# Loading the first feed-forward weights as eight loads of unequal row counts in place of four whole ones, in a one-core decode block

## The chip, the cores and the metric

The kernel runs on one core of one Trainium2 chip. The metric is the device time of one execution, in microseconds (us). The kernel before took 1313.02 us as the median of three runs (1312.45 to 1314.26). All tensors are float32.

## The reference, cut to what matters

One decode step of a transformer block, for two sequences (B = 2) and one new token each. The widths are D = 512, 32 heads of 128, a key and value cache of 8192 positions, and a feed-forward width of F = 1792.

```python
def _A_ref(x, k_cache, v_cache, wq, wo):          # x is layernorm(input)
    q = (x @ wq).reshape(B, 1, 32, 128).transpose(0, 2, 1, 3)
    scores = einsum("bhqd,bhkd->bhqk", q, k_cache) * 128 ** -0.5
    o = einsum("bhqk,bhkd->bhqd", softmax(scores), v_cache)
    return o.transpose(0, 2, 1, 3).reshape(B, 1, 4096) @ wo

def _B_ref(x, w1, b1, w2, b2):                    # x is layernorm(h)
    h = relu(x @ w1 + b1) ** 2
    return h @ w2 + b2

h  = x + _A_ref(layernorm(x), k_cache, v_cache, wq, wo)
h2 = h + _B_ref(layernorm(h), w1, b1, w2, b2)
```

The weights `wq` and `wo` have 8 MB each, `w1` and `w2` 3.67 MB each, and the two caches together 537 MB: 64 pairs of a head and a sequence with 4 MB of keys and 4 MB of values each.

## The kernel before, in words

SBUF holds a ring of three slots, each 128 partitions by 16384 floats (8 MB). One slot takes the keys and the values of one pair, or `wq`, or `wo`. The 64 pairs are worked one after the other by a loop over `i`. `front(i)` makes the scores of pair `i` with 32 matmuls (line 156), takes their maximum on VectorE (line 158) and their exponential on ScalarE (line 159). `back(i)` multiplies the values with them in four passes on VectorE of 2048 columns each, whose sums are the pair's unnormalised output (`weighted`, line 165). Every load is issued by the SyncE queue (SP), in the order of the program.

The end of the program differs from the loop. Slot 0 takes `wo`, in two halves (line 61). Pair 62, the last but one, goes to slot 1. The last pair, 63, goes to slot 2: its keys as one load (line 227), then its values as five (line 234, the fourth quarter in two parts). After the scores of pair 63 and the last pass over the values of pair 62 the program issues the feed-forward weights into slot 1. `W1`, a view of 4 blocks of 1792 columns, takes the place of the keys of pair 62: one load of 128 rows for each block (line 251), where a row is 1792 contiguous floats, 7168 bytes. `W2` is 14 blocks of 512 columns and takes the next columns of the slot, in five loads of 4, 4, 3, 2 and 1 blocks (line 254).

A load into a place must wait until the instructions that read what was there are done. Besides, the framework gives the loads eight completion semaphores in turn: load number n of the program uses semaphore n mod 8, and it is not issued before load n - 8 has landed. SP waits for this ahead of the issue, and whatever stands behind it on SP waits too. Counted in the program, the four loads of `W1` are numbers 73 to 76 and wait for pair 62 (65), the keys of pair 63 (66), the second half of `wo` (67) and the first quarter of the values of pair 63 (68). The five of `W2` are numbers 77 to 81 and wait for the second and third quarters, the two parts of the fourth, and the first load of `W1`. The store of the result is number 82 and waits for the second load of `W1`.

When the last pair is done, the tail runs: its part of the output (lines 195 and 196), the projection with `wo` (lines 203, 212 and 274), the second layernorm (lines 102 to 114), the first feed-forward matmuls, 32 records in 4 blocks of `W1` (line 281), the transposition and squared relu on VectorE (lines 287 to 292), the second feed-forward matmuls, 112 records in 14 blocks of `W2` (line 295), and the store (line 299). The first matmul of a block waits for that block's load.

Of the kernel before, what the change touches and what calls it, by code (L numbers as in the profile page):

```python
# [25 lines left out]
BLK = 512  # L26
GROUPS = [(0, 16), (16, 31), (31, 32)]
W2_PIECES = [4, 4, 3, 2, 1]
EPS = 1e-5
SCALE = DH ** -0.5  # L30

# [2 lines left out]
def attention_block_kernel(ctx: ExitStack, tc: tile.TileContext, small, kvd, wqd, wod, w1d, w2d, out):  # L34
    nc = tc.nc
# [18 lines left out]
    W1 = ring[:, 1, : DB * F].rearrange("p (d c) -> p d c", d=DB)  # L54
# [21 lines left out]
    eps_t = consts.tile([P, 1], F32, name="eps_t")  # L76
    nc.vector.memset(eps_t, EPS)
    zero = consts.tile([P, 1], F32, name="zero")
# [169 lines left out]
    sl = front(last)  # L248
    weighted(last - 1, s, NH - 1, 0, CS, AC[:, last - 1, NH - 1 : NH])
    for d in range(DB):  # L250
        nc.sync.dma_start(W1[:, d], w1d[:, d])
    at = 0
    for n in W2_PIECES:
        nc.sync.dma_start(W2[:, at : at + n], w2d[:, at : at + n])
# [75 lines left out]
```

## Time and profile before

| What | us |
|---|---|
| median of the three runs | 1313.02 |
| the profiled execution | 1314.19 |
| its span in the profile | 1312.4 |
| the DMA engines' busy share over the span | 99.0% |
| VectorE busy | 729.7 (56%) |
| TensorE busy | 415.3 (32%) |
| ScalarE busy | 143.8 (11%) |
| moved by DMA | 561 MB at 428 GB/s |

The profiled execution stands 1.8 us above its span, which is the time around the span that the profile doesn't show, and 1.17 us above the median. The chain in the profile is the chain of work that ended last, followed back from the end; where it names a DMA, the instruction behind it had waited for that load to land. A line with SPq is SP's queue, issuing or waiting. PEclk is the clock that TensorE was granted, as a share of full speed.

### The profile page before, as it was taken

What the parts mean: (1) busy time and instruction counts of PE and PEld (TensorE: products, weight loads), DVE (VectorE), ACT (ScalarE), POOL (GpSimd) and SP (SyncE); (2) the same over time, 40 slices, a digit from 0 to 9 for tenths busy, and PEclk for the clock granted to TensorE, in tenths of its full rate; (3) what the DMA queues carried; (4) which work ended last, traced back from release to release, by engine and by line L of the source; (5) the groups of instructions that cost most, each with busy time, mean ns of one, the idle gap of its engine ahead of it and who ended that gap; (6) DMA issues with size and microseconds to landing.
All of it is one profiled execution on the core that took longest, in us unless ns stands there. A gap on an engine that the chain in (4) does not pass through costs nothing.

```text
span 1312.4 us, 6090 instructions
## 1 busy us (share of the span) xinstructions
PE 415.3 (32%) x2476; PEld 121.8 (9%) x2476; DVE 729.7 (56%) x633; ACT 143.8 (11%) x149; POOL 0.7 (0%) x6
## 2 busy tenths in 40 slices
PE   3523323313322322322332332332332232233355
PEld 0300000000000000000000000000000000001113
DVE  1455665564565566466556556556556655655743
ACT  1111011011011101101101101101110110110111
POOL 0000000000000000000000000000000000000000
PEclk9666566666667666666666656656665666675766
DMA  9999999999999999999999999999999999999996
GB/s 416 416 445 428 433 445 420 441 424 439 430 430 442 425 441 430 431 434 428 436 427 441 432 433 430 437 428 433 435 432 431 434 439 422 443 429 434 428 417 265
DMA packets 11979, 561.45 MB, mean 428 GB/s; under 512 B 1456, under 2 KB 1584, under 8 KB 2736
## 3 DMA queue, kind: packets, MB, share of 16 engines
q1 hardware_dynamic: 11952, 561.07, 99.0%
q8 instruction: 19, 0.31, 0.1%
q14 instruction: 8, 0.07, 0.0%
HBM read 561.00 MB, written 0.07 MB: 428 GB/s over the span
## 4 chain that ended last, share of the span: by engine, by line
DMA 63%; DVE 20%; PE 12%; ACT 4%; issue 1%; SPq 0%; DVEq 0%; ACTq 0%
DMA ring<-in_kvd 62%; DVE ring L165 15%; PE s L156 9%; DVE NM L158 4%; ACT s L159 3%; DMA ring<-in_wqd 2%; PE s L139 1%; PE s L133 1%; PE s L203 0%; PE s L281 0%; PE s L295 0%; DVE QR L142 0%; PE s L274 0%; PE s L212 0%; ACT big L135 0%
## 5 line engine op out<-in xcount | busy, mean ns | idle before, releaser
L165 DVE SCALAR_TENSOR_TENSOR ring<-ring,s 128x2048 f32<-128x2048 f32 (+1 forms) x257 | 570.5, 2276 | 135.7 <-ACT s L159 135.7
L156 PE MATMUL s<-ring,QR 128*32 128x512 f32 x2048 | 361.8, 871 | 832.2 <-DMA ring<-in_kvd 789.5
L158 DVE TENSOR_REDUCE NM<-s 128x1 f32<-128x2048 f32 x64 | 146.7, 2292 | 382.6 <-PE s L156 382.6
L159 ACT ACTIVATE s<-s,NM 128x2048 f32<-128x2048 f32 x64 | 124.3, 1942 | 1081.5 <-DVE NM L158 1081.5
L156 PEld LDWEIGHTS s<-ring,QR 128*32 128x32 f32 x2048 | 91.1, 153 | 1100.4 <-issue 1093.5
L142 DVE TENSOR_SCALAR QR<-s 128x2048 f32<-128x2048 f32 x1 | 2.3, 2291 | 38.5 <-PE s L139 38.5
L165 DVE DVE_READ_ACCUMULATOR ring<-ring,s 128x1 f32 x257 | 21.4, 83 | 0.0
L133 PE MATMUL s<-ring,xn 128*2 128x512 f32 x64 | 8.9, 703 | 18.8 <-DMA ring<-in_wqd 18.0
L203 PE MATMUL s<-ring,OT 128*2 128x512 f32 x62 | 11.6, 900 | 9.8 <-ACT s L97 5.9
L159 ACT ACTIVATION_READ_ACCUMULATOR s<-s,NM 128x1 f32 x64 | 12.3, 193 | 0.0
L139 PE MATMUL s<-ident,big 128*128 128x2 f32 x64 | 10.9, 307 | 0.8 <-ACT big L135 0.8
L139 PEld LDWEIGHTS s<-ident,big 128*128 128x128 f32 x64 | 10.8, 270 | 1.7 <-issue 1.7
L184 PE MATMUL s<-lw,pick_all 128*128 128x32 f32 (+2 forms) x6 | 1.9, 394 | 14.6 <-DVE lw L183 14.6
L97 ACT ACTIVATE s<-zero 128x512 f32<-128x512 f32 (+2 forms) x6 | 3.2, 532 | 19.8 <-DVE OT L196 10.7
L281 PE MATMUL s<-ring,xc 128*2 128x448 f32 x32 | 5.0, 794 | 0.4 <-ACT rstd L113 0.4
L176 PE MATMUL s<-NM,pick 128*128 128x32 f32 (+2 forms) x24 | 4.0, 310 | 3.3 <-DVE hT L213 2.6
L176 PEld LDWEIGHTS s<-NM,pick 128*128 128x128 f32 x24 | 3.7, 236 | 5.3 <-issue 3.5
L135 ACT ACTIVATE big<-s 128x512 f32<-128x512 f32 x2 | 1.2, 598 | 26.8 <-PE s L133 26.8
L103 PE MATMUL s<-part,ones_d 128*128 128x2 f32 x8 | 2.3, 363 | 5.2 <-ACT s L97 3.4
L133 PEld LDWEIGHTS s<-ring,xn 128*2 128x2 f32 x64 | 1.6, 92 | 25.2 <-issue 23.5
L203 PEld LDWEIGHTS s<-ring,OT 128*2 128x2 f32 x62 | 2.0, 110 | 18.9 <-issue 12.1
L295 PE MATMUL s<-ring,a 128*2 128x128 f32 x112 | 3.2, 273 | 1.4 <-DVE a L292 1.4
(59 smaller groups left out, 38.4 us busy)
## 6 DMA issues: line engine op xcount, KB each, us to landing
ring<-in_wod SPq DMA_DIRECT2D x2, 4096.0 KB, 42.1
ring<-in_kvd SPq DMA_DIRECT2D x1, 4096.0 KB, 32.7
ring<-in_w1d SPq DMA_DIRECT2D x4, 896.0 KB, 20.3
ring<-in_kvd SPq DMA_DIRECT2D x3, 1024.0 KB, 38.5
ring<-in_w2d SPq DMA_DIRECT2D x2, 1024.0 KB, 16.6
ring<-in_kvd SPq DMA_DIRECT2D x2, 512.0 KB, 38.3
ring<-in_kvd SPq DMA_DIRECT2D x63, 38.9
ring<-in_w2d SPq DMA_DIRECT2D x1, 768.0 KB, 17.6
```

What stands on the lines that cost most here:

```text
L97: nc.scalar.activation(ap, zero.to_broadcast([P, n]), AF.Copy)
L103: nc.tensor.matmul(pm, ones_d, part, start=True, stop=True)
L133: nc.tensor.matmul(bk[k][32 * j : 32 * j + B, :], xn[:, d, :], WQ[:, d, n * BLK : (n + 1) * BLK], start=(d == 0), stop=(d == DB - 1))
L139: nc.tensor.matmul(bk[2][:, h * B : (h + 1) * B], big[:, at : at + DH], ident[:, 32 * j : 32 * j + B], start=True, stop=True)
L156: nc.tensor.matmul(bk[n][32 * j : 32 * j + 32, :], QR[:, i, :], keys(i)[:, j, n * BLK : (n + 1) * BLK], start=True, stop=True)
L158: nc.vector.tensor_reduce(NM[:, i : i + 1], s, axis=AX.X, op=ALU.max, negate=True)
L159: nc.scalar.activation(s, s, AF.Exp, bias=NM[:, i : i + 1], scale=1.0, accum_out=LS[:, i : i + 1])
L165: nc.vector.scalar_tensor_tensor(v, v, 1.0, s[:, lo:hi], op0=ALU.mult, op1=ALU.mult, accum_out=acc)
L176: nc.tensor.matmul(pn[:, j], pick[:, j, :], NM[:, a:b], start=True, stop=True)
L203: nc.tensor.matmul(hp[32 * j : 32 * j + B, :], OT[:, h * B : (h + 1) * B], WO[:, h, :], start=(h - h0 < NQ), stop=(h1 - h <= NQ))
L281: nc.tensor.matmul(y[32 * j : 32 * j + B, :], xc[:, d, :], W1[:, d, j * FQ : (j + 1) * FQ], start=(d == 0), stop=(d == DB - 1))
L295: nc.tensor.matmul(o[32 * j : 32 * j + B, :], a2[:, m, :], W2[:, m, j * P : (j + 1) * P], start=False, stop=(m == FB - 1))
```

## The change

Each of the four loads of `W1` is issued as two, cut by rows (partitions): rows 0 to 119 and 120 to 127 of the first block, 104 and 24 rows of the second, 88 and 40 of the third, 72 and 56 of the fourth. The bytes, their places and the order of the blocks stay. No compute instruction is added or removed.

```diff
 W2_PIECES = [4, 4, 3, 2, 1]
+W1_CUTS = [120, 104, 88, 72]
...
     for d in range(DB):
-        nc.sync.dma_start(W1[:, d], w1d[:, d])
+        cut = W1_CUTS[d]
+        nc.sync.dma_start(W1[:cut, d], w1d[:cut, d])
+        nc.sync.dma_start(W1[cut:, d], w1d[cut:, d])
     at = 0
     for n in W2_PIECES:
         nc.sync.dma_start(W2[:, at : at + n], w2d[:, at : at + n])
```

With four loads more, the numbers behind the first of them move, and with them the semaphores. In the program after, `W1` is loads 73 to 80, which wait for loads 65 to 72: pair 62, the keys of pair 63, the second half of `wo`, and the five loads of the values of pair 63. `W2` is loads 81 to 85, which wait for the first five loads of `W1` (120, 8, 104, 24 and 88 rows), and the store waits for the sixth (40 rows). On TensorE the first matmul of each block of line 281 waits for two loads in place of one. The order of the instructions on each engine is otherwise the same.

## The prediction

> **What bounds the kernel now.** I read the page first: the span, the DMA row of the slices and the shares of the chain.
>
> ```profile
> span 1312.4 us, 6090 instructions
> DMA  9999999999999999999999999999999999999996
> DMA 63%; DVE 20%; PE 12%; ACT 4%; issue 1%; SPq 0%; DVEq 0%; ACTq 0%
> ```
>
> The DMA engines are full until the last fortieth, so the loop is bound by the caches' 537 MB. The change touches nothing issued before load 73, so only the end counts. There the chain in order of time shows which wait ends last:
>
> ```profile
> 1226.67 29.79 DMA ring<-in_kvd
> 1256.46 0.14 issue
> 1256.59 6.54 PE s L156 x32
> ...
> 1287.14 4.49 DVE ring L165 x6
> ...
> 1299.46 5.03 PE s L281 x32
> 1304.49 0.27 PE s L285 x8
> ...
> 1305.91 0.20 DVE a L292
> 1306.11 0.04 issue
> 1306.15 3.28 PE s L295 x112
> ```
>
> The last DMA on the chain is pair 62, landing at 1256.46. From there to the end it is 53 us of compute: neither line 281 (`W1`) nor line 295 (`W2`) follows a DMA. Third, the queue: SP's timeline, then its own waits from 1250 us on.
>
> ```profile
> 1263.03 15.77 SPq L251 DMA_DIRECT2D ring<-in_w1d  x4
> 1280.96 7.48 SPq L254 DMA_DIRECT2D ring<-in_w2d  x5
> ```
>
> ```profile
> SPq L251 <- DMA ring<-in_kvd: 13.8, 3, 8.9
> SPq L254 <- DMA ring<-in_kvd: 6.0, 4, 2.1
> SPq L299 <- DMA ring<-in_w1d: 1.8, 1, 1.8
> SPq L254 <- DMA ring<-in_w1d: 1.8, 1, 1.8
> ```
>
> SP issues each load late, when the load eight before it lands. Last, the stretches of the tail (columns: busy time of PE, PEld, DVE, ACT, POOL, then granted clock, DMA share, GB/s):
>
> ```profile
> 1292.00:1296.00 4.00, 3.24 (x22) 3.10 (x22) 0.34 (x3) 0.00 (x0) 0.00 (x0) 0.50 1.00 416
> 1296.00:1300.00 4.00, 2.49 (x12) 1.80 (x16) 1.01 (x7) 0.26 (x1) 0.00 (x0) 0.50 0.81 328
> 1300.00:1302.00 2.00, 2.00 (x16) 0.44 (x12) 0.00 (x0) 0.00 (x0) 0.00 (x0) 0.50 0.45 174
> 1302.00:1304.00 2.00, 2.00 (x20) 0.43 (x16) 0.00 (x0) 0.00 (x0) 0.00 (x0) 0.70 0.10 41
> 1304.00:1306.00 2.00, 0.71 (x16) 0.13 (x8) 1.11 (x4) 0.00 (x0) 0.00 (x0) 1.00 0.00 0
> ```
>
> The transfers don't stop together: the share falls from 1.00 to 0.81, 0.45 and 0.10, so some DMA engines are done about 5 us before the others, and all are idle by 1304.3, ahead of line 295.
>
> **Cover of each load.** Asked load by load, the four issues of line 251 start at 1263.0, 1266.2, 1276.0 and 1278.5 and land 25.1, 24.1, 16.5 and 16.2 us later: 1288.1, 1290.3, 1292.5, 1294.7. Line 281 takes a block of `W1` every 5.03/4 = 1.26 us from 1299.46, the fourth at 1303.2, so the covers are 11.4, 10.4, 9.5 and 8.5 us. The five issues of line 254 land at 1297.1, 1300.5, 1302.3, 1303.6 and 1304.2 (the last 1288.1 + 16.1). Line 295 takes 3.28 us for 14 blocks and reaches the pieces (after 0, 4, 8, 11, 13 blocks) at 1306.15, 1307.1, 1308.0, 1308.7, 1309.2. Covers: 9.0, 6.6, 5.7, 5.1 and 5.0 us. The smallest, 5.0 us of the last piece, is what the change may use up for nothing.
>
> **The change part by part.**
>
> *Four more issues on SP*, 0.33 us each by line 251's records: 1.3 us. Behind them on SP stand only `W2` and the store, and SP spends these stretches waiting. Nothing.
>
> *The issues of `W2` come later.* The first piece now waits for the 120-row load instead of the second value quarter: about 1288.1 instead of 1281.0, if the 120 rows land when the first block did. The fifth waits for the 88-row load, at about the third block's landing, 1292.5, plus what the loads ahead gained; before it was 1288.1. A queue that runs dry costs time. At 1288.1 the engines that are behind still have three blocks queued: 2.75 MB at 428 GB/s is 6.4 us, and an issue to an idle queue lands after 1.5 us (the store's row). At the fifth issue they still have a third of a block and the fourth, about 2.8 us. So the engines that finish last never run dry; one with few rows of `W1` may, but from 1289.6 it needs only 3.67 MB at 428 GB/s, 8.6 us, for all of `W2`, and is done by 1299 or so. Nothing.
>
> *The store* waits for the sixth load of `W1`, before 1300 in every case below but the dear one, against 1309.8. Nothing.
>
> *Four more waits on TensorE*, ahead of line 281's blocks, for loads long landed. Low end nothing, since the waits can run ahead of the pipelined matmuls; high end the 0.14 us "issue" behind a DMA wait at line 156, 0.6 us together. I take 0.1: the other "issue" rows are 0.02 to 0.04.
>
> *The rows on the DMA engines.* Bytes are the same, but a load that isn't 128 rows need not fill sixteen engines evenly. The trace of before has no such load, so I bound it. At 428/16 = 26.75 GB/s per engine a 7168-byte row takes 0.268 us; a block is 8 rows per engine, all of `W1` 32. Low end: still 32, nothing (an engine that is late may even get fewer, but an earlier landing is worth nothing under cover). High end: the larger load keeps 8 rows on an engine and the smaller one puts another 8 on that same engine, four times: 64 rows, 32 x 0.268 = 8.6 us more. I take the smaller loads spread as the 128-row ones are: 1 + 2 + 3 + 4 rows on the busiest engine, 42 in all, 10 x 0.268 = 2.7 us, because every load that the trace shows completes in sixteen parts. Then the last `W1` lands at 1297.4 (needed 1303.2) and the last of `W2` at 1306.9 (needed 1309.2): 2.3 us of cover are left, and the end doesn't move. At the high end the last piece lands at 1312.8 and the end moves 3.6 us.
>
> [...]
>
> **Sum.** 0.1 us, from the waits on TensorE. The profiled execution would go from 1314.19 to 1314.3; the median of the runs lies 1.17 us below it: 1313.1, which I round up to 1313.2.
>
> **The rivals.**
>
> *Slower: the cut loads move more slowly, and the last piece of `W2` comes too late.* [...] For it: at 1.00 DMA share and 26.75 GB/s per engine nothing is to spare, and no row shows an unevenly shared load. Against it: the five value loads and `W2` pieces of four sizes all keep that rate. If each row took twice as long, 42 rows would be 22.5 us in place of 8.6: 13.9 more, less 5.0 of cover, 8.9 us, 1322. Between no slowing and that, the high end of the row count alone gives 3.6 us, 1316.7. It decides from 5.0 us of extra work on the engine that ends last, and passes 0.2% (2.6 us) from 7.6: `W1` taking 16.2 us there in place of 8.6. Chance 0.26, around 1317.
>
> [...]
>
> *Faster: TensorE gets its clock earlier in the tail.* In the stretches above it is granted 0.50 until 1302, and 1.00 only from 1304. Line 281's 5.03 us at nearly half clock could become 2.5, and lines 212 and 274 (1.88 each) half: 4.4 us at most, 1308.8. Against it: the change gives the clock no cause, and the spread of the three runs, 1.8 us, contains such luck already. With 2.6 us needed, chance 0.1. The same luck the other way (line 295 at half clock, 3.3 us, 1316.4) has 0.04.
>
> *The cut changes nothing in the engines' shares*: the forecast again, 1313.0, and inside it.
>
> **How the numbers follow.** A difference below 0.2%, 2.6 us, is about what a measurement of this kernel can't tell from none. Forecast and the do-nothing case, 0.60: 1313.2, within 1311.5 and 1315. Slower rival 0.26 and late clock 0.04 give slower 0.30; faster 0.10. The range goes up to 1318.0, over the high end of the rows (1316.7) and part of the slowing, leaving out 0.1, and down to 1310.8, leaving out 0.07.
>
> **What would show it.** Right: SP's timeline has eight issues at line 251/254 of the new kernel from 1263 on; the first `W2` issue moves to about 1288; the DMA share decays longer, with 1304 to 1307 not at zero; TensorE's `W2` matmuls still follow VectorE on the chain, 53 us after pair 62's landing. Wrong: the chain shows a DMA ahead of `W1`'s or `W2`'s matmuls; `W1` rows that take much more than 0.27 us; or a chain that differs before 1263, which I hold untouched.

## The result, and the profile after

The changed kernel takes 1326.84 us (median of four runs, 1325.96 to 1327.29) against 1313.36 us for the kernel before (median of the three runs of the table and one more): 1.010 times as long, 95% interval 1.0088 to 1.0112, or 13.5 us more. The forecast was 1313.2 in a range of 1310.8 to 1318.0. The profiled execution took 1326.43 us at a span of 1324.7, 12.3 more than the span before.

The page of the kernel after: the span, the slices, and the chain by line.

```profile
span 1324.7 us, 6097 instructions
DMA  9999999999999999999999999999999999999996
GB/s 412 434 422 440 439 420 438 441 420 437 438 432 430 435 438 429 429 438 432 428 437 430 432 441 428 439 428 433 434 435 427 434 437 426 431 441 423 432 351 179
DMA ring<-in_kvd 58%; DVE ring L166 16%; PE s L157 11%; DVE NM L159 4%; ACT s L160 4%; DMA ring<-in_wqd 2%; DMA ring<-in_w1d 2%; DMA ring<-in_w2d 2%; PE s L134 1%; PE s L140 1%; DVE QR L143 0%; ACT big L136 0%; PE s L298 0%; PE s L185 0%; SPq L59 0%
```

`W1` and `W2` are new on the chain. The last two slices move 351 and 179 GB/s (417 and 265 before), while the row above still calls the DMA engines full in the last but one. The chain in order of time, from the last value loads on:

```profile
1241.88 36.79 DMA ring<-in_kvd
1278.67 0.02 issue
1278.68 21.94 DMA ring<-in_w1d
1300.63 0.02 issue
1300.64 20.11 DMA ring<-in_w2d
1320.76 0.04 issue
1320.80 0.62 PE s L298 x16
```

Three transfers follow each other, tied by SP's semaphores: a value load lands at 1278.67 and lets the 24-row load go, that lands at 1300.63 and lets the fourth `W2` load go. Before, 53 us of compute stood here. The timeline of TensorE and of SP's queue, with one line of VectorE (start, duration, in brackets the idle time ahead and what ended it):

```profile
1262.56 0.40 SPq L253 DMA_DIRECT2D ring<-in_w1d  x1
...
1290.99 0.32 SPq L254 DMA_DIRECT2D ring<-in_w1d  x1
1291.00 1.22 DVE L166 SCALAR_TENSOR_TENSOR ring<-ring,s 128x1024 f32<-128x1024 f32 x1 [1.18 <-DMA ring<-in_kvd]
...
1294.75 12.03 SPq L257 DMA_DIRECT2D ring<-in_w2d  x5
1300.07 3.17 PE L284 MATMUL s<-ring,xc 128*2 128x448 f32 x16 [0.41 <-ACT rstd L114]
...
1308.23 1.68 PE L284 MATMUL s<-ring,xc 128*2 128x448 f32 x8 [4.98 <-DMA ring<-in_w1d]
...
1312.87 1.67 PE L284 MATMUL s<-ring,xc 128*2 128x448 f32 x8 [2.97 <-DMA ring<-in_w1d]
...
1316.41 3.97 PE L298 MATMUL s<-ring,a 128*2 128x128 f32 x88 [1.44 <-DVE a L295]
...
1320.80 1.03 PE L298 MATMUL s<-ring,a 128*2 128x128 f32 x24 [0.42 <-DMA ring<-in_w2d]
```

TensorE waits 4.98 and 2.97 us for the third and fourth blocks of `W1`. This gives the account of the span. The first `W1` matmul starts 0.6 us later (1299.46, now 1300.07); ahead of it VectorE had waited 1.18 us for the last values of pair 63. From there to the first `W2` matmul it is 16.34 us in place of 6.69, 9.65 more, of which 7.95 are the two waits; the rest fits matmuls that stay at half clock (a granted clock of 0.50 in every stretch of 4 us from 1288 to 1316, where the kernel before had 0.70 from 1302 and 1.00 from 1304). From the first `W2` matmul to the copy of the result it is 5.49 us in place of 3.31, 2.2 more. Together 12.4. The stretches show why the loads are late (the last three columns are granted clock, DMA share and GB/s). First one of the kernel before, then those of the kernel after:

```profile
1284.00:1288.00 4.00, 1.64 (x10) 1.47 (x10) 2.91 (x7) 2.35 (x5) 0.00 (x0) 0.77 1.01 418
```

```profile
1284.00:1288.00 4.00, 1.13 (x7) 0.96 (x7) 3.01 (x7) 2.40 (x5) 0.00 (x0) 0.62 0.97 219
1292.00:1296.00 4.00, 2.63 (x19) 2.49 (x19) 0.87 (x6) 0.00 (x0) 0.00 (x0) 0.50 0.93 191
1300.00:1304.00 4.00, 3.17 (x16) 0.40 (x16) 0.17 (x1) 0.02 (x1) 0.00 (x0) 0.50 1.01 192
1316.00:1320.00 4.00, 3.59 (x84) 2.52 (x87) 0.33 (x2) 0.00 (x0) 0.00 (x0) 0.62 0.14 53
```

The DMA engines are about as busy as before (0.93 to 1.01 up to 1304) and move half as much: 191 to 219 GB/s in these, 176 between 1288 and 1292, where the stretches 1284 to 1288 and 1292 to 1296 had 418 and 416. In the DMA records of the packed trace, which hold the start and the duration of each row's transfer, a row of `W1` took 276 ns on average before (287 at most) and 539 after (900 at most).

### The profile page after: what moved, and what is told of

Its sections match the earlier page's. It is cut to its first block, busy times and chain, and to the rows that moved or that the text cites. A ratio compares the mean times of both kernels' runs of the same rounds, so it can differ in the third digit from the quotient of the medians.

```text
span 1324.7 us, 6097 instructions
## 1 busy us (share of the span) xinstructions
PE 427.2 (32%) x2476; PEld 123.1 (9%) x2476; DVE 729.7 (55%) x633; ACT 143.7 (11%) x149; POOL 0.7 (0%) x6
## 4 chain that ended last, share of the span: by engine, by line
DMA 63%; DVE 20%; PE 13%; ACT 4%; issue 0%; SPq 0%; DVEq 0%
DMA ring<-in_kvd 58%; DVE ring L166 16%; PE s L157 11%; DVE NM L159 4%; ACT s L160 4%; DMA ring<-in_wqd 2%; DMA ring<-in_w1d 2%; DMA ring<-in_w2d 2%; PE s L134 1%; PE s L140 1%; DVE QR L143 0%; ACT big L136 0%; PE s L298 0%; PE s L185 0%; SPq L59 0%
## 5 line engine op out<-in xcount | busy, mean ns | idle before, releaser
L157 PE MATMUL s<-ring,QR 128*32 128x512 f32 x2048 | 370.8, 890 | 823.7 <-DMA ring<-in_kvd 686.9
L134 PE MATMUL s<-ring,xn 128*2 128x512 f32 x64 | 9.9, 775 | 18.9 <-DMA ring<-in_wqd 18.1
L160 ACT ACTIVATION_READ_ACCUMULATOR s<-s,NM 128x1 f32 x64 | 12.3, 193 | 0.0
```

The source lines that it names most:

```text
L134: nc.tensor.matmul(bk[k][32 * j : 32 * j + B, :], xn[:, d, :], WQ[:, d, n * BLK : (n + 1) * BLK], start=(d == 0), stop=(d == DB - 1))
L157: nc.tensor.matmul(bk[n][32 * j : 32 * j + 32, :], QR[:, i, :], keys(i)[:, j, n * BLK : (n + 1) * BLK], start=True, stop=True)
L160: nc.scalar.activation(s, s, AF.Exp, bias=NM[:, i : i + 1], scale=1.0, accum_out=LS[:, i : i + 1])
```

## The experiments

Two kinds of experiments were made, each a change to the kernel before. In those called e the loads of `W1` are cut in another way. In those called m, `W1` is left whole and one load of the loop is cut, the 8 MB of pair 30, where the DMA engines are the bound (99.0% busy over the span) and the cost lies bare. (Two of the expectations call it pair 33; the loads of both runs are pair 30.) The m runs are single runs beside 1313.43 us (m1, m3; the median of 13 runs) and 1311.93 us (m5 to m8; one run) for the kernel before; the others have intervals.

**Is it the eight loads and their semaphores?** (e2_columns)

```diff
-        nc.sync.dma_start(W1[:, d], w1d[:, d])
+        nc.sync.dma_start(W1[:, d, : F // 2], w1d[:, d, : F // 2])
+        nc.sync.dma_start(W1[:, d, F // 2 :], w1d[:, d, F // 2 :])
```

> Each block of W1 as two halves by columns, 128 rows of 896 each: eight loads, and W2 and the store wait for the same numbers of loads as in the change, but each load spans all 128 rows. Queue: about 1326.8. Rows and collisions: 1313.4 within 0.2%, since every engine gets 8 rows of each load as before.

1313.10 us, ratio 0.9997 (0.9987 to 1.0007). SP's line of the `W2` loads:

```profile
1287.10 4.78 SPq L255 DMA_DIRECT2D ring<-in_w2d  x5
```

Eight loads in the same turn, with `W2` issued from 1287.1 to 1291.9 in place of 1281.0 to 1288.4, cost nothing. The queue theory falls, and so does the thought that the change's four more waits on TensorE matter.

**Are 64 rows slower?** (e1_halves on `W1`, m1_halves in the loop)

```diff
-        nc.sync.dma_start(W1[:, d], w1d[:, d])
+        nc.sync.dma_start(W1[:64, d], w1d[:64, d])
+        nc.sync.dma_start(W1[64:, d], w1d[64:, d])
```

> Each block of W1 as rows 0 to 63 and rows 64 to 127: eight loads as in the change, in the same turn of the semaphores, but every load has 64 rows, which sixteen engines can share evenly. Three theories of the 13.5 us. Rows (the busiest DMA engine has more rows): 32 rows on each engine as before, so 1313.4, no change. Queue (with eight loads the loads of W2 are issued late): the same queue as after, so about 1326.8. Collisions (DMA engines that write into neighbouring partitions at the same time slow each other): at half rate W1 takes 17.2 us in place of 8.6, 8.6 more less 5.0 of cover: 1317.0, and 0.26 to 0.30% over before.

```diff
+        if i == 30:
+            nc.sync.dma_start(slot(i)[:64], kvd[i][:64])
+            nc.sync.dma_start(slot(i)[64:], kvd[i][64:])
+            return
         nc.sync.dma_start(slot(i), kvd[i])
```

> Only the load of pair 33, 8 MB in the middle of the loop, is issued as rows 0 to 63 and 64 to 127; W1 is loaded whole. There the DMA engines are the bound, so its cost is bare. Before, a load lands every 19.35 us. Rows and queue: no change, 1313.4. Collisions at half rate: 19.35 us more, 1332.7.

m1 took 1335.82 us, 22.4 more, near the 19.35 of the half rate. A stretch of it inside the cut load:

```profile
620.00:630.00 10.00, 0.00 (x0) 0.00 (x0) 6.45 (x6) 0.00 (x0) 0.00 (x0) 0.50 1.00 211
```

Engines full, 211 GB/s. In the DMA records the 64 KB rows that began between 606 and 642 us took 5.07 us on average, where the kernel before has 2.42. Sixteen equal shares of the 128 rows at 5.07 us would be 40.6 us, an estimate that fits the 40.8 us from the start of the scores of the pair ahead (607.76) to that of pair 30's (648.55), each of which waits for its load. e1 took 1321.26, ratio 1.0062 (1.0047 to 1.0077), 7.8 us more where half rate was priced at 3.6. The chain of e1 from its last value load:

```profile
1249.31 41.53 DMA ring<-in_kvd
1290.84 0.02 issue
1290.86 16.50 DMA ring<-in_w1d
1307.35 0.04 issue
1307.40 1.68 PE s L282 x8
...
1310.94 5.88 PE s L296 x112
```

The last part of the values of pair 63 lands at 1290.84 in place of 1285.9, although the first of the five value loads still lands at 1278.5 (1278.4 before): the end of what was already under way is slowed when the first loads of `W1` go beside it. So `W1` is late for this as well as for its own rate, and its fourth block lands at 1307.35, 4.1 us after 1303.2, when it was needed before; `W2`'s matmuls then take 5.88 us in place of 3.28.

**120 and 8 rows** (m3_120_8, the same edit with 120 for 64)

> Only the load of pair 33 is issued as rows 0 to 119 and 120 to 127. Rows: a row of 64 KB takes 2.42 us in an engine, and one engine has 9 in place of 8, or 16 if both loads begin on the same one: 2.4 to 19.4 us more, with 2.4 taken: 1315.8. Queue: 1313.4. Collisions: the 120 rows at down to half rate, so 10 to 24 us more: 1323 to 1337.

1346.97 us, 33.5 more, outside all of it. The 2.4 of the rows theory is refuted, and the cut costs more than a halved rate of the 120 rows can explain. In the DMA records the rows that began between 602 and 638 us took 4.97 us on average, as with the halves; the 32 rows that began between 638 and 654, at the end of the cut load and the start of the next, took 8.12, up to 10.81.

**Which rows may share a load?** (m5_32_64_32, m6_32_32_64, m7_eighths; the lines stand in the same `if i == 30:` as in m1, and m7 has eight loads of 16 rows there)

```diff
+            nc.sync.dma_start(slot(i)[0:32], kvd[i][0:32])
+            nc.sync.dma_start(slot(i)[32:96], kvd[i][32:96])
+            nc.sync.dma_start(slot(i)[96:128], kvd[i][96:128])
```

> The load of pair 30 as three: rows 0 to 31, 32 to 95, 96 to 127. [...] Rival, any load under 128 rows goes at half rate: 38.7 us, 19.4 more or the 22.4 of the halves, 1333 to 1336. Rival, the number of loads: three cost more than the two halves, over 1336. [...]

```diff
+            nc.sync.dma_start(slot(i)[0:32], kvd[i][0:32])
+            nc.sync.dma_start(slot(i)[32:64], kvd[i][32:64])
+            nc.sync.dma_start(slot(i)[64:128], kvd[i][64:128])
```

> The same three sizes with the 64 rows at the end: rows 0 to 31, 32 to 63, 64 to 127. [...] Sizes or number of loads: the same time as with the 64 rows in the middle.

> The load of pair 30 as eight of 16 rows. [...] Half rate for whatever isn't 128 rows: 1333 to 1336 at most.

m5 took 1327.57 (15.6 more), m6 1335.94 (24.0 more), m7 1359.54 (47.6 more). The same three sizes differ by 8.4 us with the place of the 64 rows. In the DMA records the rows that began between 618 and 622 us took 2.45 us on average in m5, when its middle load went, and 4.95 in m6, which still moved 210 GB/s from 630 to 640, when by these rates its 64 rows went: rows 32 to 95 are not slow, rows 64 to 127 are. The theory under test, that the place of the rows sets a load's rate (the paths of e3 and e5), had the place right and the sizes not: with the 64 middle rows at the 428 GB/s of before (9.7 us) and the two loads of 32 rows at half rate (9.7 us each) my estimate was 1323.1 for m5, 4.5 too little, and 10 to 13 us between the two runs. The stretch 620 to 630 of m5, m6 and m7, one line each:

```profile
620.00:630.00 10.00, 0.00 (x0) 0.00 (x0) 7.42 (x8) 0.00 (x0) 0.00 (x0) 0.50 1.13 308
```

```profile
620.00:630.00 10.00, 0.00 (x0) 0.00 (x0) 6.74 (x8) 0.00 (x0) 0.00 (x0) 0.50 1.00 211
```

```profile
620.00:630.00 10.00, 0.00 (x0) 0.00 (x0) 8.66 (x8) 0.00 (x0) 0.00 (x0) 0.50 1.16 157
```

m6 moves what the halves moved, m5 more (the stretch holds the end of the middle load and the start of the last), and sixteen neighbouring rows less: 131 to 157 GB/s in the stretches from 620 to 660, between a quarter and a half of 428. The rows of m7 that began between 606 and 656 us took 7.71 us on average, 3.2 times 2.42. Both rivals, half rate for any load under 128 rows and a price by the number of loads, fail on m5 against m6, and the first on m7 too.

**Reading or writing side?** (m8_evenodd)

```diff
+            nc.sync.dma_start(slot(i)[0:128:2], kvd[i][0:64])
+            nc.sync.dma_start(slot(i)[1:128:2], kvd[i][64:128])
...
+    kv[30] = np.concatenate([kv[30][0::2], kv[30][1::2]])
```

> The load of pair 30 as two of 64 rows that lie in HBM as before, 64 neighbouring rows for each load, but go to the even partitions and then to the odd ones (the rows of that pair are laid out in HBM to suit). [...] Reading side is the cause: the 1335.8 of the halves again. [...]

1312.65 us, 0.7 more than the run beside it, which is within the spread of the kernel before.

```profile
620.00:630.00 10.00, 4.19 (x28) 1.30 (x32) 3.94 (x4) 0.00 (x0) 0.00 (x0) 0.56 1.00 433
```

433 GB/s: two loads of 64 rows at the full rate, read from HBM (the chip's main memory) exactly as the halves of m1. So the slowing lies where the rows are written, not where they are read, and it isn't the number of rows. My expectation of some slowing, 1320 to 1330, was wrong.

**The same repair on `W1`** (e3_evenodd)

```diff
-        nc.sync.dma_start(W1[:, d], w1d[:, d])
+        nc.sync.dma_start(W1[0:128:2, d], w1d[:64, d])
+        nc.sync.dma_start(W1[1:128:2, d], w1d[64:, d])
```

(On the host the rows of `W1` are laid out to suit.)

> Each block of W1 as two loads of 64 rows, to the even partitions and to the odd ones (the rows of W1 are laid out in HBM to suit): eight loads, issued in the same turn as the change's. Paths: full rate as with the one even and odd pair in the loop, so 1313.2 within 0.2%. If the tail had another cause beside (eight loads, fewer rows in a load), it shows here: 1321 as with the halves.

1313.33 us, ratio 1.0001 (0.9992 to 1.0011). Eight loads of 64 rows, each spread evenly over all partitions, cost nothing; the same sizes on neighbouring rows cost 7.8 us.

**What makes the change dearer than the halves?** (e5_120_8, e4_96_32, e6_88_40, e7_72_56, e8_80_48, e9_104_24; the edit of e1 with another number)

> All four blocks of W1 as 120 and 8 rows. This asks what made the change (13.5 us) dearer than the halves (7.8). Paths with uneven rows: in the loop the halves of an 8 MB load cost 22.4 us and 120 and 8 rows 33.6; W1 has 3.67 of 8.39 MB, so 9.8 and 14.7 us. The halves of W1 cost 7.8, so 2.0 stayed under cover, and 120 and 8 should cost 12.7: 1326.1. If uneven rows do not count and only the halved rate does: 1321, as with the halves.

> All four blocks of W1 as 96 and 32 rows, both of them whole multiples of sixteen, so no engine needs to have more rows than another. [...] Uneven rows as the sole cause: 1313.2.

> All four blocks of W1 as 88 and 40 rows, to find what makes the change 5.1 us dearer than three other cuts that all came to 1321.3 to 1321.8. [...] At half rate a row is 0.54 us: 48 rows are 8.6 us over the 1321.5 of the even cuts, 1330, and dearer than the change. Rate theory, no count of rows matters and only the mixture of the change's four cuts is bad: 1321 to 1322 as the other cuts.

> All four blocks of W1 as 72 and 56 rows. Rows theory: 12 engines of 6 and 14 of 4, so 40 rows on the busiest, 8 more than the even cuts, 4.3 us at half rate: 1325.8, close to the change. Rate theory: 1321 to 1322.

> All four blocks of W1 as 80 and 48 rows, a cut between the two dear ones (72 and 56, 88 and 40: 1326.8 and 1327.6), but both counts are multiples of sixteen, as with the halves and with 96 and 32 (1321.3 and 1321.7). Shares theory: the cut is dear where a load's rows do not go evenly onto sixteen engines, so 1321 to 1322. [...]

> All four blocks of W1 as 104 and 24 rows. [...] Place theory: the cut lies between 96 and 120, which both were 1321.7, so 1321 to 1322.

The rows on the busiest engine are an estimate: the rows of a load over the parts in which it landed, for an engine that has a part of every load. The landing records of the change show 15, 8, 13, 12, 11, 10, 12 and 14 parts for its loads of 120, 8, 104, 24, 88, 40, 72 and 56 rows; for the counts that are multiples of sixteen I take 16 parts, as the whole loads had. Beside them the measured times (GB/s is that of the stretch 1284 to 1304):

| rows of the two loads | rows on the busiest engine (estimate) | us | ratio, 95% interval | GB/s |
|---|---|---|---|---|
| 64 and 64 | 32 | 1321.26 | 1.0062 (1.0047 to 1.0077) | 235 |
| 96 and 32 | 32 | 1321.66 | 1.0063 (1.0048 to 1.0078) | 234 |
| 80 and 48 | 32 | 1322.26 | 1.0070 (1.0054 to 1.0087) | 217 |
| 120 and 8 | 36 | 1321.75 | 1.0062 (1.0047 to 1.0077) | 228 |
| 104 and 24 | 40 | 1323.18 | 1.0078 (1.0063 to 1.0093) | 212 |
| 72 and 56 | 40 | 1326.83 | 1.0105 (1.0088 to 1.0122) | 207 |
| the change | 41 | 1326.84 | 1.0100 (1.0088 to 1.0112) | 197 |
| 88 and 40 | 48 | 1327.59 | 1.0110 (1.0095 to 1.0125) | 200 |

Three of the four forecasts that gave uneven rows a price missed: 1326.1 for 120 and 8 (scaled from the loop; its rival, that uneven rows don't count, gave 1321 and fits), 1330 for 88 and 40, and the dear group, 1326 to 1327.5, for 104 and 24; 1325.8 for 72 and 56 came within 1.0 us. The theory of the place alone missed too, with 1326 to 1328 for 80 and 48, which lies between the two dear cuts and is cheap. What stands: all three cuts into multiples of sixteen rows cost 7.8 to 9.8 us; the dearest cuts, at 13.5 to 15.0 us, are all among the others, but a row has no fixed price, since 36 rows cost nothing clear of the noise beside 32, and 40 came out at 1323.2 and at 1326.8. The cut into 96 and 32 rows came to 1321.66, as dear as the halves, although its larger load lies in both halves of the partitions, as the middle load of m5 did (2.45 us a row); why, no run shows. How place and shares act together is seen in part in the DMA records. Rows on the busiest engine times the mean duration of a `W1` row in that run (0.48 to 0.54 us, over all engines) give, in the order of the table, 15.7, 16.3, 16.9, 17.3, 19.4, 21.0, 22.1 and 23.3 us, and the last `W1` row ends in the same order: 1306.3, 1307.0, 1307.3, 1308.0, 1309.2, 1311.88, 1311.95 and 1312.2. This fits a slower row and a count that multiply. No run was made to test it, it doesn't give the sizes exactly (7.6 us between the first and the last, against 5.9), and what sets a row's duration between 0.48 and 0.54 stays open.

No run was faster than the kernel before; the two forms that cost nothing, by columns and by even and odd rows, are as fast.

## Why the prediction was wrong

**The step that failed is "The rows on the DMA engines".** It priced a row at 0.268 us whatever load it belongs to and let only the count of rows vary, so that its high end, 8.6 us more, left 3.6 at the end. The count was the lesser part: in m1 and e1 it is the old one by the estimate of sixteen equal shares, and m1 runs at 211 GB/s, e1 at 7.8 us more. The row's duration changed: 276 ns became 539 on average.

**Why.** Loads whose rows all lie in the same half of the partitions, rows 0 to 63 or rows 64 to 127, went at half of the 428 GB/s of before or less: 211 and 210 GB/s at a DMA share of 1.00 and 1.02 for the halves (m1, 620 to 630 and 630 to 640), 4.95 us a row in m6 against 2.45 for rows 32 to 95 (m5), and 131 to 157 GB/s for sixteen neighbouring rows (m7). The slowing lies with the writing: even and odd partitions went at 433 GB/s (m8) and cost nothing on `W1` (e3, 1313.33, against 1321.26 of e1). That the engines get in each other's way there, and wait for each other, is inferred from these rates and places; what would make them wait no run shows. In the change, whose larger loads reach into both halves, a row took 539 ns all the same.

**The rival, that the cut loads move more slowly, was right and was given too small a price and chance (0.26).** It reckoned 42 rows at double duration, 13.9 us more, took off the 5.0 us of cover of `W2`'s last piece, and came to 1322, with a range that stopped at 1318. The doubling itself was right on average: the 41 rows of the estimate x 0.539 are 22.1 us, where it had 22.5. Two terms were missing. The first is the loads that are already under way: the last value load of pair 63 landed 5.0 us later (1290.97 by the landing records, 1285.93 before), so `W1` lands 18.1 us later, at 1312.8 instead of 1294.7, near 13.9 + 5.0. The second is the wrong cover: not only `W2`'s last piece was short, but `W1`'s third and fourth blocks, whose 9.5 and 8.5 us of cover were used up. TensorE stood still there, and `W2`'s matmuls, which had run at a granted clock of 1.00, now did so only from about 1319 on (0.62 on average in the stretch from 1316 to 1320); they and their last waits took the 2.2 us more.

**"The issues of `W2` come later" was right that this costs nothing by itself** for issues from 1287.1 to 1291.9 (e2), and wrong in the moment: 1294.75 instead of 1288, because the 120-row load landed 6.6 us later than the whole block had. Whether issues as late as the change's, up to 1306.8, add something to the slow rows no run shows apart.

**The waits on TensorE and the issues on SP cost nothing**, as taken: e2 and e3 have them all, at 0.9997 and 1.0001.

**The untouched part was untouched**: the first load of `W1` was issued at 1262.56 (1263.03 before), and pair 62's scores began at 1256.88 (1256.59).

**The count of rows rose too, and was the smaller part of the cost.** The landing records (one entry for each part of a load that lands) have 16 parts for each whole load of `W1` before; for the eight loads after they have 15, 8, 13, 12, 11, 10, 12 and 14, beside one entry at the issue of each. So not every load lands in sixteen parts, as the prediction took it from the loads of before. Rows over parts give an estimate of 41 rows on the busiest engine in place of 32, where the prediction had 42; which engine took which rows no record shows. The 2.7 us for ten rows more was a sum at the old rate; at 0.539 us a row the nine rows more are 4.9 us, near the 5.6 by which the change is dearer than the halves.

## What to carry to other kernels

Cutting a load into neighbouring rows changed its rate here, not only its size: cut by columns, or into even and odd rows, each part is spread over all partitions and the cut cost nothing here (433 GB/s for the even and odd rows in the loop); cut into neighbouring halves, both went at half of that (211). Read the GB/s of a stretch beside its DMA share: a share of 1.00 with half the bytes was the sign that the rows themselves had become slower. And cover counted in microseconds holds only at the rate it was counted at, for every load under way at the same time.

## What the runs showed that was not expected

Two loads to even and odd partitions run at full rate, 433 GB/s, with their rows at 2.42 us in the DMA records, as before. An 8-row load after one of 120 rows cost 33.5 us in the loop, for the same 8 MB that two halves move at 22.4. On `W1` the same pair of cuts costs nearly alike (1321.75 and 1321.26), though its last row there ended 1.7 us later; why the loop parts the two by so much more the runs don't explain.
